# Attention and a two-layer network on one core: second parts of the first token columns on GpSimd, and the last weight ticks spread over four slots

## The chip, the core and the metric

The kernel runs on one core of one Trainium2 chip. The metric is device time in microseconds (us) of one launch. A core has five engines with a queue each: TensorE (PE in the profile; its weight loads are PEld), VectorE (DVE), ScalarE (ACT), GpSimd (POOL) and SyncE (SP), which here issues every DMA. Each engine works through its own list of instructions in order, and waits for the others through semaphores.

## What is computed

The reference is causal attention with a decay, and then a normalised two-layer network with a residual:

```python
# q, k, v: 8 batches x 8 heads x 576 tokens x 64; f: 8 x 8 x 576
scores = q @ k.T / 8 + cum[:, None] - cum[None, :]     # cum = cumsum(log f); causal mask
attn   = exp(scores - max) / (sum + 1e-9)
x      = (attn @ v)                                    # heads side by side: 8 x 576 x 512
xn     = (x - mean) / sqrt(var + 1e-6) * g_ln
out    = x + relu(xn @ w_ch1) @ w_ch2                  # 512 -> 2048 -> 512
```

The network's weights come as 64-bit floats, everything else as 32-bit floats.

## The kernel before

**Slots.** The attention is 64 heads of four slots each, slot `(n, t)` with t from 1 to 4, in all 256; a slot handles one tile of 128 query rows (t = 1 also a corner tile of 64). The body of a slot is a string of letters, one per piece of work, in the table `ORDERS`; the order of the letters is the order in which instructions are written out, and so their order on each engine. In slots 37 to 65 the string is (before that the same pieces stand in a somewhat other order, `R` near the end) `WwQSstAMhPelgNFrfmBDLRba`. The pieces that matter here are: `W` ticks of the weight preparation; `Q` scores on TensorE (L374); `S` mask and row minimum on VectorE (L409); `e` the exponential on ScalarE (L420); `B` the reciprocal of the row sum on VectorE (L425, L426) and the scaling of the row on GpSimd (L427); `t` the transposes on TensorE (L448) of the tile of two slots ago, which read what L427 wrote; `h` their copies on ScalarE (L504); `A` attention times values (L518); `F` copies of its result (L575, L576); `M` and `N` a step of the network's first and second layer on TensorE (L622 to L624, L644 to L646), with `r` and `m` the relu in two parts on ScalarE and VectorE (L630, L635); `P` preparation, `D` loads for later heads, `L` some steps of the reciprocal square root on GpSimd (L707 to L715), `R` the loads and splits of the network's token columns.

**Two-part numbers.** A 32-bit number is split for the matmuls into a first part (a rounded copy, by ScalarE) and a second part (the rest, by a subtraction). For the network's token columns `chunk_split` does this: L606 on ScalarE, then L607 on VectorE. A chunk is 256 tokens with four such column tiles `x_0` to `x_3`, and 16 steps of the first layer; chunk 0 is split at the ends of slots 36 and 37, and its first step is in slot 38. Two buffers `xr` hold the loaded columns, so the load of `x_2` waits until `x_0` is split.

**Weight preparation.** `WPrep` turns 32 pieces of weights (two layers, 16 each) into first and second parts, `w1h` with `w1l` and `w2h` with `w2l`. A tick moves every piece in work one step on. Per piece that is a load, a scaling on ScalarE (L166), three bit operations of 128x512 on VectorE (L182, L186, L189), for the first layer column sums on TensorE (L201) and four centring operations on VectorE (L209), then the first part on ScalarE (L225) and the second on GpSimd (L229). `W` runs ticks as they fall due: 0.8 per slot from slot 34 on. What is left in slot 56 (head 14, t = 1) is run there at once, in piece `P`, in a loop until all 37 ticks are done.

**Buffers.** The weight preparation's tiles are in a pool `early`. When it is done the pool is closed, and a pool `late` is opened in the same space; it holds the tiles of the heads from 16 on, which are split in two parts (`raw`, `hi`, `pw` and others). Heads 0 to 15 are computed in full precision and need none of it. TensorE's results go to banks of the PSUM memory; six banks of one tag are handed round among scores, transposes, products, column sums and first-layer steps, and a matmul waits until the bank that it gets has been read.

## Time and profile before

| what | value |
| --- | --- |
| device time, median of 3 runs | 1217.96 us (1214.26 to 1219.36) |
| the profiled execution's own time | 1217.98 us |
| its span, first to last instruction | 1216.1 us |
| mean granted TensorE clock | 0.993 |
| busy: TensorE, VectorE, ScalarE, GpSimd | 1190.1, 757.0, 619.3, 452.6 us |
| TensorE instructions (matmul) | 8368 |

The profiled execution's time is 1.9 us above its span and within 0.02 us of the median. In a row of the timeline or the chain the first number is the start in us, the second how long it took, then engine, line, operation, and the tiles it writes and reads; in square brackets stands how long the engine was idle before, and whose end ended that. A row of the table of windows has a stretch, its length, and for each engine the busy time in it with the number of instructions, then the clock granted to TensorE (1.00 is full speed), the share of the DMA engines and GB/s.

### The profile page before, as it was taken

What the parts mean: (1) busy time and instruction counts of PE and PEld (TensorE: products, weight loads), DVE (VectorE), ACT (ScalarE), POOL (GpSimd) and SP (SyncE); (2) the same over time, 40 slices, a digit from 0 to 9 for tenths busy, and PEclk for the clock granted to TensorE, in tenths of its full rate; (3) what the DMA queues carried; (4) which work ended last, traced back from release to release, by engine and by line L of the source; (5) the groups of instructions that cost most, each with busy time, mean ns of one, the idle gap of its engine ahead of it and who ended that gap; (6) DMA issues with size and microseconds to landing.
All of it is one profiled execution on the core that took longest, in us unless ns stands there. A gap on an engine that the chain in (4) does not pass through costs nothing.

```text
span 1216.1 us, 25716 instructions
## 1 busy us (share of the span) xinstructions
PE 1190.1 (98%) x8368; PEld 1068.3 (88%) x8368; DVE 757.0 (62%) x2664; ACT 619.3 (51%) x1936; POOL 452.6 (37%) x768
## 2 busy tenths in 40 slices
PE   8888998999999999999999999999999999999998
PEld 6557887899999989999999999999999999999997
DVE  6777683477777767777767676767677752222122
ACT  6886574555555555555555555556555541112111
POOL 3543344454444434454534344445444410000000
PEclk9998998999999999999999999999999999999999
DMA  6454452243434344434344444434444421111100
GB/s 192 142 153 151 127 148 63 87 133 131 139 125 143 123 141 131 146 129 135 124 129 141 129 135 131 143 120 139 132 132 131 128 86 41 31 36 39 31 26 27
DMA packets 127541, 139.00 MB, mean 114 GB/s; under 512 B 32432, under 2 KB 100016, under 8 KB 127408
## 3 DMA queue, kind: packets, MB, share of 16 engines
q1 hardware_dynamic: 127408, 137.36, 36.6%
q8 instruction: 67, 1.10, 0.4%
q14 instruction: 66, 0.54, 0.1%
HBM read 79.61 MB, written 19.17 MB: 81 GB/s over the span
## 4 chain that ended last, share of the span: by engine, by line
PE 91%; DVE 3%; ACT 2%; DMA 1%; issue 1%; POOL 1%; SPq 0%; DVEq 0%; ACTq 0%; POOLq 0%
PE h L622 12%; PE h L624 11%; PE h L623 11%; PE acc L644 11%; PE acc L645 11%; PE acc L646 11%; PE o L543 6%; PE tr L446 4%; PE s L376 3%; PE s L377 3%; PE s L374 2%; PE o L518 2%; PE tr L448 1%; ACT p L420 1%; DVE p L409 1%
## 5 line engine op out<-in xcount | busy, mean ns | idle before, releaser
L427 POOL TENSOR_SCALAR p<-p,st 64x64 f32<-64x64 f32 (+4 forms) x320 | 169.9, 532 | 511.5 <-ACT ph L504 232.4
L622 PE MATMUL h<-x,w1h 128*128 128x256 f32 x1152 | 342.3, 297 | 0.4 <-DVE st L409 0.4
L624 PE MATMUL h<-x,w1l 128*128 128x256 f32 x1152 | 326.8, 284 | 0.0
L623 PE MATMUL h<-x,w1h 128*128 128x256 f32 x1152 | 326.3, 283 | 0.0
L420 ACT ACTIVATE p<-p,st 64x64 f32<-64x64 f32 (+4 forms) x320 | 179.2, 561 | 210.6 <-DVE st L409 206.0
L635 DVE SCALAR_TENSOR_TENSOR hh<-h,hh 128x256 fp32r<-128x256 f32 x288 | 120.5, 418 | 194.4 <-ACT hh L630 192.0
L644 PE MATMUL acc<-w2h,hh 128*128 128x512 f32 x576 | 228.4, 397 | 0.0
L645 PE MATMUL acc<-w2l,hh 128*128 128x512 f32 x576 | 227.8, 396 | 0.0
L646 PE MATMUL acc<-w2h,hh 128*128 128x512 f32 x576 | 225.5, 391 | 0.0
L622 PEld LDWEIGHTS h<-x,w1h 128*128 128x128 f32 x1152 | 219.6, 191 | 5.3 <-issue 0.9
L623 PEld LDWEIGHTS h<-x,w1h 128*128 128x128 f32 x1152 | 220.6, 192 | 2.5
L624 PEld LDWEIGHTS h<-x,w1l 128*128 128x128 f32 x1152 | 220.3, 191 | 0.0
L630 ACT ACTIVATE hh<-h 128x256 fp32r<-128x256 f32 x288 | 109.9, 381 | 184.5 <-PE h L624 184.2
L409 DVE CUSTOM_DVE_ANT_0 p<-s,mask 64x64 f32<-64x64 f32 (+4 forms) x320 | 132.2, 421 | 26.4 <-PE s L377 17.7
L646 PEld LDWEIGHTS acc<-w2h,hh 128*128 128x128 f32 x576 | 108.5, 188 | 24.7
L425 DVE TENSOR_SCALAR st<-st 128x1 f32<-128x1 f32 (+1 forms) x320 | 47.7, 149 | 120.2 <-ACT p L420 117.2
L644 PEld LDWEIGHTS acc<-w2h,hh 128*128 128x128 f32 x576 | 109.5, 190 | 14.0 <-ACT ph_full L504 0.2
L645 PEld LDWEIGHTS acc<-w2l,hh 128*128 128x128 f32 x576 | 109.5, 190 | 11.7
L504 ACT CAST ph<-tr 64x128 fp32r<-64x128 f32 (+4 forms) x384 | 107.2, 328 | 3.6 <-PE tr L446 1.3
L579 ACT COPY ot<-o 64x320 f32<-64x320 f32 x96 | 38.0, 396 | 125.5 <-PE tr L446 63.7
L509 DVE TENSOR_TENSOR pl<-tr,ph 128x128 fp32r<-128x128 f32 x192 | 88.0, 458 | 4.3
L377 PE MATMUL s<-kl,xq 66*128 66x288 f32 (+4 forms) x288 | 83.2, 297 | 0.0
(89 smaller groups left out, 1888.7 us busy)
## 6 DMA issues: line engine op xcount, KB each, us to landing
raw<-in_qk_dram SPq DMA_DIRECT2D x96, 288.0 KB
wr<-in_w_dram SPq DMA_DIRECT2D x32, 512.0 KB
pw<-p SPq DMA_DIRECT2D x48, 288.0 KB
pw<-p SPq DMA_DIRECT2D x48, 224.0 KB
vr<-in_v_dram SPq DMA_DIRECT2D x64, 160.0 KB
out_dram<-xt SPq DMA_DIRECT2D x36, 256.0 KB
pw<-p SPq DMA_DIRECT2D x48, 160.0 KB
xa<-xs SPq DMA_DIRECT2D x32, 160.0 KB
```

The source lines that it names most:

```text
L377: mm(sp, xq, kl, start=False, stop=True)
L409: nc.vector.tensor_tensor_reduce(out=pt[:m, a:z], in0=sp, in1=mask[:m, off + a : off + z], scale=-SCALE, scalar=3.0e38 if i == 0 else st[: ...
L420: nc.scalar.activation(pt[:m, :w], pt[:m, :w], AF.Exp, bias=st[:m, i : i + 1], scale=-1.0, accum_out=st[:m, 2:3])
L427: nc.gpsimd.tensor_scalar(out=pt[:m, :w], in0=pt[:m, :w], scalar1=st[:m, 3:4], scalar2=1.0, op0=ALU.mult, op1=ALU.mult)
L622: mm(ph, w1h[:, k, fs], c.x[k][:, 0, :], start=(k == 0), stop=False)
L623: mm(ph, w1h[:, k, fs], c.x[k][:, 1, :], start=False, stop=False)
L624: mm(ph, w1l[:, k, fs], c.x[k][:, 0, :], start=False, stop=(k == KT - 1))
L630: nc.scalar.activation(h[:, 0, :], c.ph, AF.Relu)
L635: nc.vector.scalar_tensor_tensor(out=h[:, 1, :], in0=ph, scalar=0.0, in1=h[:, 0, :].bitcast(F32), op0=ALU.max, op1=ALU.subtract)
L644: mm(c.acc[i], h[:, 0, ts_], w2h[:, j, :], start=(j == 0), stop=False)
L645: mm(c.acc[i], h[:, 0, ts_], w2l[:, j, :], start=False, stop=False)
L646: mm(c.acc[i], h[:, 1, ts_], w2h[:, j, :], start=False, stop=(j == FT - 1))
```

## The change

`chunk_split` puts the subtraction on GpSimd as long as the pool `late` isn't open. The loop over the remaining ticks moves out of `P` of slot 56: piece `D` of slots 56, 57 and 58 now runs up to two ticks each, with all that they queue, and `D` of slot 59 runs what is left, closes `early`, opens `late` and issues the first of head 16's two `raw` loads. The second is issued in `D` of slot 60. Before, they were issued in `D` of slots 57 and 58.

```diff
+W_CLOSE = 2
...
         nc.scalar.copy(out=x[:, 0, :], in_=xr)
-        nc.vector.tensor_tensor(out=x[:, 1, :], in0=xr, in1=x[:, 0, :].bitcast(F32), op=ALU.subtract)
+        eng = nc.gpsimd if "late" not in pools else nc.vector
+        eng.tensor_tensor(out=x[:, 1, :], in0=xr, in1=x[:, 0, :].bitcast(F32), op=ALU.subtract)
...
         def next_raw():
 
-            if slot is not None and t in (2, 3) and NFULL <= n + 2 < B * H:
+            if slot is None:
+                return
+            if n == NFULL - 2:
+                ticks = W_CLOSE if t < 4 else 99
+                while not wp.done() and ticks > 0:
+                    wp.tick()
+                    wp.fill(99)
+                    ticks -= 1
+                if t == 4:
+                    early.close()
+                    pools["late"] = ctx.enter_context(tc.tile_pool(name="late", bufs=1))
+                    start_head(NFULL)
+                    load_raw(hd[NFULL], 1)
+            elif n == NFULL - 1 and t == 1:
+                load_raw(hd[NFULL], 0)
+            elif t in (2, 3) and NFULL < n + 2 < B * H:
                 if t == 2:
                     start_head(n + 2)
                 load_raw(hd[n + 2], 1 if t == 2 else 0)
...
                 if t == 1 and n + 1 < NFULL:
                     start_head(n + 1)
-                if n == NFULL - 2 and t == 1:
-                    while not wp.done():
-                        wp.tick()
-                        wp.fill(99)
-                    early.close()
-                    pools["late"] = ctx.enter_context(tc.tile_pool(name="late", bufs=1))
```

TensorE's list of instructions is the same before and after, row by row. On VectorE six subtractions of 128x256 go (chunk 0's four and chunk 1's first two), and they come up on GpSimd. The lines of the changed kernel stand one to two further down (L607 is now L609, L229 is L230, L427 is L428, L325 is L326, L723 is L725, L409 is L410, L182 is L183).

VectorE's list at the first split of chunk 0, from the end of slot 36 into slot 37; `st` are row statistics, `y_8` is a bit operation of the weights, `p_2` the masked scores of the tile `s_2`. Before:

```order
L425 TENSOR_SCALAR st_1_1348<-st_1_1348 128x1
L426 RECIPROCAL st_1_1348<-st_1_1348 128x1
L607 TENSOR_TENSOR x_0_1380<-xr_0_1326,x_0_1380 128x256
L607 TENSOR_TENSOR x_1_1383<-xr_1_1328,x_1_1383 128x256
L182 TENSOR_SCALAR y_8_1396<-wr_8_1264 128x512
L409 ISA p_2_1400,st_2_1401<-s_2_0_1398,mask 128x320
```

GpSimd's list at the same place in the changed kernel:

```order
L428 TENSOR_SCALAR p_1_1347<-p_1_1347,st_1_1348 128x192
L609 TENSOR_TENSOR x_0_1380<-xr_0_1326,x_0_1380 128x256
L609 TENSOR_TENSOR x_1_1383<-xr_1_1328,x_1_1383 128x256
L230 TENSOR_TENSOR w1l<-wy_6_989,w1h 128x4x128
L428 TENSOR_SCALAR p_2_1400<-p_2_1400,st_2_1401 128x320
L609 TENSOR_TENSOR x_2_1423<-xr_2_1386,x_2_1423 128x256
L609 TENSOR_TENSOR x_3_1426<-xr_3_1388,x_3_1426 128x256
L230 TENSOR_TENSOR w2l<-wy_7_1243,w2h 128x512
```

VectorE goes from the reciprocal straight to the bit operation and the scores of `s_2`; on GpSimd each pair of subtractions stands behind a row scaling and ahead of a weight's second part.

GpSimd's list where the weight preparation ends, from slot 56 on; `rs` are steps of the reciprocal square root. Before:

```order
L229 TENSOR_TENSOR w2l<-wy_14_2224,w2h 128x512
L229 TENSOR_TENSOR w1l<-wy_14_2138,w1h 128x4x128
L229 TENSOR_TENSOR w2l<-wy_15_2329,w2h 128x512
L229 TENSOR_TENSOR w1l<-wy_15_2285,w1h 128x4x128
L427 TENSOR_SCALAR p_0_175<-p_0_175,st_0_2436 64x64
L427 TENSOR_SCALAR p_1_2438<-p_1_2438,st_1_2439 128x192
L712 TENSOR_TENSOR rs_2154<-rs_2154 128x2
```

The same place in the changed kernel:

```order
L230 TENSOR_TENSOR w2l<-wy_14_2224,w2h 128x512
L428 TENSOR_SCALAR p_0_175<-p_0_175,st_0_2436 64x64
L428 TENSOR_SCALAR p_1_2438<-p_1_2438,st_1_2439 128x192
L230 TENSOR_TENSOR w1l<-wy_14_2138,w1h 128x4x128
L230 TENSOR_TENSOR w2l<-wy_15_2329,w2h 128x512
...
L428 TENSOR_SCALAR p_2_2490<-p_2_2490,st_2_2491 128x320
L230 TENSOR_TENSOR w1l<-wy_15_2285,w1h 128x4x128
```

The row scalings of slot 56 now stand behind one second part in place of four; the last second part, `w1l` of piece 15, stands behind the row scaling of slot 57 and six `rs` steps. ScalarE's `L225` for piece 15 likewise moves from ahead of slot 56's exponentials to behind them.

SyncE's list of DMAs from slot 57 on, `xb` being a store of attention's result, `vr` a load of values and `out_dram` the store of chunk 0. Before:

```order
L325 DMA raw_1_2528<-in_qk_dram 128x576
L332 DMA vr_2566<-in_v_dram 128x5x64
L325 DMA raw_0_2583<-in_qk_dram 128x576
L592 DMA xb_156<-xs_320_2377 128x256
L723 DMA out_dram<-xt_0_2151 128x512
L723 DMA out_dram<-xt_1_2394 128x512
L341 DMA kl_2720<-cumd 2x576
```

In the changed kernel:

```order
L333 DMA vr_2560<-in_v_dram 128x5x64
L593 DMA xb_156<-xs_320_2377 128x256
L326 DMA raw_1_2622<-in_qk_dram 128x576
L725 DMA out_dram<-xt_0_2151 128x512
L725 DMA out_dram<-xt_1_2394 128x512
L326 DMA raw_0_2689<-in_qk_dram 128x576
L342 DMA kl_2720<-cumd 2x576
```

Both `raw` loads stand later, the second one now behind the two stores of chunk 0.

## The prediction

> **What bounds it now.** I read first the page's busy times and the granted clock, then the table of windows for the first 203 us, in which the change lies.

> ```profile
> PE 1190.1 (98%) x8368; PEld 1068.3 (88%) x8368; DVE 757.0 (62%) x2664; ACT 619.3 (51%) x1936; POOL 452.6 (37%) x768
> core 0: 1216.1 us, clock 0.993
> 0.00:203.20 203.20, 181.42 (x1259) 142.86 (x1260) 144.50 (x517) 139.22 (x426) 87.07 (x137) 0.96 0.49 143
> ```

> TensorE bounds the kernel: it is busy 98% of the span. Of its 26.0 us of idle time, 21.8 (203.20 - 181.42) lie in the first 203 us; after that it is idle 4.2 us in 1013. The clock is 0.96 in this stretch. So an edit pays if it lets TensorE reach 203 us earlier, and what it gains there arrives at the end. The change touches two places before 203 us and nothing that TensorE waits for later.

> A clock of 0.993 is a loss of 8.5 us of full-speed time (0.007 x 1216.1). The windows, cut where the clock steps, show where:

> ```profile
> 93.99:97.40 3.41, 2.39 (x14) 1.65 (x13) 3.23 (x14) 2.49 (x7) 1.56 (x2) 0.99 0.35 93
> 97.40:100.81 3.41, 3.41 (x22) 3.03 (x20) 2.60 (x11) 2.37 (x8) 1.93 (x2) 0.51 0.71 212
> 100.81:104.23 3.42, 1.52 (x10) 0.88 (x7) 2.91 (x8) 3.38 (x11) 2.19 (x4) 0.99 0.53 146
> 104.23:107.64 3.41, 2.67 (x7) 1.86 (x8) 3.38 (x12) 1.81 (x5) 0.56 (x1) 0.50 0.69 212
> 107.64:111.05 3.41, 3.41 (x25) 3.01 (x24) 2.87 (x7) 1.75 (x5) 1.48 (x2) 0.51 0.41 137
> 189.55:192.96 3.41, 0.98 (x4) 0.26 (x3) 1.27 (x7) 1.43 (x6) 3.41 (x4) 0.99 0.13 48
> 192.96:196.38 3.42, 2.66 (x19) 2.06 (x20) 0.00 (x0) 1.14 (x4) 2.93 (x12) 0.50 0.31 86
> 196.38:199.79 3.41, 3.41 (x19) 3.08 (x16) 0.00 (x0) 0.52 (x2) 0.18 (x1) 0.51 0.35 93
> ```

> Three times a window of 3.41 us with little TensorE work (2.39, 1.52, 0.98 us busy) is followed by half clock: one window the first time, two windows the second and third, since the window after the drop is itself not full (2.67, 2.66). Five windows at half are 17.1 us, or 8.5 lost, which is all of it. The second and third are the two places of the change, and each hangs on one wait. I call them A (chunk 0's first split) and B (the end of the weight preparation).

> **A, the split on GpSimd.** The chain of waits at 102 us, and TensorE's timeline:

> ```profile
> 101.79 0.44 PE tr L448 x4
> 102.23 0.12 PE tr_4b L448
> 102.43 1.48 DVE x L607
> 103.91 0.60 DVE y L182
> 104.52 0.39 DVE p L409
> ...
> 104.97 1.86 PE L374 MATMUL s<-kl,xf 66*128 66x448 f32 x2 [2.63 <-DVE st L409]
> ...
> 111.25 0.38 PE L622 MATMUL h<-x,w1h 128*128 128x256 f32 x1
> ```

> TensorE waits 2.63 us for the masking of `s_2` (L409), which stands on VectorE behind two L607 and an L182. Their times:

> ```profile
> 101.45 0.16 DVE L426 RECIPROCAL st<-st 128x1 f32<-128x1 f32 x1
> 102.06 1.85 DVE L607 TENSOR_TENSOR x<-xr,x 128x256 fp32r<-128x256 f32 x2 [0.44 <-ACT x L606]
> 103.83 0.68 DVE L182 TENSOR_SCALAR y<-wr 128x512 uint32<-128x512 uint32 x1
> ...
> 102.20 1.43 POOL L229 TENSOR_TENSOR w1l<-wy,w1h 128x512 fp32r<-128x512 f32 x1
> 107.08 0.80 POOL L427 TENSOR_SCALAR p<-p,st 128x320 f32<-128x320 f32 x1 [3.45 <-DVE st L426]
> L607 DVE TENSOR_TENSOR x<-xr,x x72: 411/424/1484, 102.1 to 1164.6; 128x256 fp32r<-128x256 f32 x72
> ```

> Without the two L607, L182 starts when the reciprocal ends, at 101.61 in place of 103.83: 2.22 us sooner, the 0.44 of waiting included. Then `s_3` starts at 102.75 instead of 104.97, TensorE idles 0.4 us, and the window to 104.23 holds 2.95 us of work (1.52 + 1.43). The drops above came after 2.39 us and less (the windows with 2.67 and 2.66 were at half already), so I take it that the clock stays full. The work from 104.97 to 111.25, 6.28 us at half, then takes half of that, 3.14. The bounds of A: 2.2 us if the clock falls all the same for as long, 5.4 (2.22 + 3.14) if nothing else is late. Not all will be on time: the column sum's readers (L209) stand behind the reciprocal of slot 37, which waits for ScalarE, and the product L518 waits on VectorE. ScalarE is full in that window (3.38 of 3.42). I take off 1.0 for that: **A = 4.4 us**.

> What moves to GpSimd costs there, per 128x256 subtraction, an estimate between 0.72 (half of the 128x512 subtraction at 102.20, 1.43) and 1.43 (a whole one); nothing of this form is on GpSimd now. I take 0.72, since twice the elements should be twice the work. Two of them fill 102.2 to 103.7 and push `w1l` there to about 105.1; GpSimd idles 3.45 us before its next row scaling, so that is hidden. The second pair comes behind that scaling, at about 106 to 107.4 on the new clock, and the first step's matmuls reach `x_2` and `x_3` 0.8 and 1.2 us after their start at 106.8: on time by some tenths. If that cover is gone, each tenth costs TensorE a tenth. The load of `x_2`, which waits for the split of `x_0`, is issued 0.4 us later, that of `x_3` a little sooner. Chunk 1's two subtractions (0.42 us each by the last row) I count at nothing: they come after the half clock of A, where VectorE has room (2.87 of 3.41 us).

> [...]

> **B, the ticks spread.** GpSimd, TensorE and what TensorE takes at full speed for the same kinds of work:

> ```profile
> 188.42 1.30 POOL L229 TENSOR_TENSOR w2l<-wy,w2h 128x512 fp32r<-128x512 f32 x1
> ...
> 192.12 1.26 POOL L229 TENSOR_TENSOR w1l<-wy,w1h 128x512 fp32r<-128x512 f32 x1
> 193.36 0.71 POOL L427 TENSOR_SCALAR p<-p,st 64x64 f32<-64x64 f32 x2
> ...
> 195.59 0.53 POOL L427 TENSOR_SCALAR p<-p,st 128x320 f32<-128x320 f32 x1
> 189.61 0.92 PE L374 MATMUL s<-kl,xf 66*128 66x448 f32 x2
> 193.72 1.04 PE L448 MATMUL tr<-identr,p 128*64 128x128 f32 x3 [3.20 <-POOL p L427]
> ...
> 197.03 0.58 PE L622 MATMUL h<-x,w1h 128*128 128x256 f32 x1
> ...
> 199.75 0.40 PE L644 MATMUL acc<-w2h,hh 128*128 128x512 f32 x1
> ...
> 202.37 0.36 PE L622 MATMUL h<-x,w1h 128*128 128x256 f32 x1
> ```

> TensorE wants slot 56's rows at 190.53 and gets them at 193.72, since their scaling stands behind four L229. In the change one L229 is ahead: the scalings run at 189.7 to 190.4, before TensorE asks. That removes 3.20 us of idle time; and the work from 193.72 to 199.75, 6.03 us at half clock, takes 3.0. So the next second-layer matmul comes at about 193.6 in place of 199.75. I take **B = 6.0 us**, between 3.2 (the clock falls all the same) and 6.2.

> What is late next: the second parts themselves. `w1l` of piece 14 ends at 191.7, and the step that needs it comes at 192.2 (190.53 and half of the 3.31 us from 193.72 to 197.03). `w1l` of piece 15 stands behind six `rs` steps (194.04 to 195.59 now, 1.55 us) and slot 57's scaling (0.53): 190.4 + 2 x 1.26 + 1.55 + 0.53 + 1.26 = 196.3, and step 15 comes at 196.2 (193.6, and the 2.62 us from 199.75 to 202.37), its third matmul, the first to read `w1l`, some 0.2 later. Slot 57's scaling ends at 195.0, and its transposes come just ahead of step 15. All hold, the tightest by a tenth. ScalarE's two casts (L225) go behind slot 56's exponentials, which come sooner for it; the steps that read what they write are two slots away and more. VectorE's four L209 likewise change places with four short row operations.

> The loads: SyncE now holds `raw_1` behind a store and `raw_0` behind the two stores of chunk 0.

> ```profile
> 193.40 0.33 SPq L325 DMA_DIRECT2D raw<-in_qk_dram  x1
> 197.76 0.62 SPq L325 DMA_DIRECT2D raw<-in_qk_dram  x1
> 210.45 1.00 SPq L723 DMA_DIRECT2D out_dram<-xt  x2
> 211.95 0.68 ACT L342 CAST hi<-raw 128x576 fp32r<-128x576 f32 x1
> 215.71 0.67 ACT L348 CAST hi<-raw 128x576 fp32r<-128x576 f32 x1
> ```

> `raw_1` can't be issued before the last `w1l` ends (196.3), and ScalarE reads it about 6 us before 211.95, that is at 206. `raw_0` follows the stores at 211.5 on the old clock and is read at 215.71: 4.2 us for 800 KB with the stores' 512, or 190 GB/s, where windows above moved 212 (their last number). So this holds with little to spare, at no cost; uncovered, ScalarE would wait a microsecond, with two slots between it and TensorE. The loads and stores that they are moved past (`vr`, `xb`) only go sooner.

> **The sum.** Profiled execution 1217.98 - 4.4 - 6.0 = 1207.6; with three tenths for the tight places, **1208 us**. The median of the runs is the same as this execution's time, so no correction.

> **Rivals.** (1) *The clock falls at A all the same* (0.12). For it: the first drop came after a window with as much as 2.39 us. It would cost 1.7 (one window at half) to 3.1 of A: 1209.5 to 1211. [...]

> (2) *VectorE takes A's gain back* (0.13): it is busy in 2.9 to 3.4 us of each window at A, and if it bounds the stretch up to 186 us, only B is left: 1212. Against it: at 107.64 to 111.05 it already has room (2.87 of 3.41). (3) *The last second parts take the stall's place* (0.1): if `w1l` 15 is over a microsecond late, step 15 waits, and a window may go to half: B shrinks to 2 to 4, 1210 to 1213. (4) *It doesn't matter* (0.05): TensorE finds both waits again behind ScalarE: 1216 to 1219. (5) *Slower* (0.04): `raw_0` lands so late behind the stores that ScalarE stops, with the exponentials behind it, and TensorE runs dry with the clock at half behind it. It decides once the landing is more than two slots late (about 10 us, by the 5.3 us between the two L622 under B); to end above 1224 it has to cost 16 us beyond that, a landing after about 241 on the old clock. No row shows a load that slow.

> **Chances.** The forecast has 0.56. I call faster what is below 1211.9 (0.5%, 6.1 us, about what a measurement here can tell from no change): the forecast, rival 1 and half of rivals 2 and 3, 0.79, less 0.03 for what I don't see: 0.76. Same 0.19: the rest of 2 and 3, rival 4, and 0.02 of that. Slower 0.05: rival 5 and 0.01 of it. The range is 1204 (both gains at their upper bounds, 5.4 + 6.2, and two more for a third clock drop that a shifted phase avoids) to 1213.5 (B alone with its clock half kept).

> **What would show it.** Right: no idle time of over 1 us before TensorE's L374 and L448 near 103 and 190; a granted clock of 0.998 to 0.999, with one half window left; GpSimd's split near 0.7 us; the first L622 near 106.8, the L644 near 189; the same 4 us of idle time after that. Wrong: half clock behind 104; a wait of TensorE for GpSimd at L623 or L624; a wait of ScalarE for `raw`.

## The result, and the profile after

The changed kernel takes 1208.47 us (median of 6 runs, 1207.64 to 1213.36) against 1217.47 for the kernel before, run beside it. The ratio is 0.9941, with a 95% interval of 0.9919 to 0.9963. The prediction was 1208.0. The profiled execution took 1208.30 us, where that of before took 1217.98.

The page's busy times, the clock, and the windows that answer to those of before:

```profile
PE 1187.0 (98%) x8368; PEld 1066.3 (88%) x8368; DVE 752.9 (62%) x2658; ACT 619.4 (51%) x1936; POOL 456.6 (38%) x774
```

```profile
core 0: 1206.5 us, clock 0.997
```

```profile
0.00:203.20 203.20, 188.35 (x1329) 149.86 (x1330) 145.81 (x529) 145.50 (x446) 93.32 (x148) 0.98 0.50 145
203.20:1206.50 1003.30, 998.69 (x7041) 916.45 (x7039) 607.12 (x2129) 473.87 (x1491) 363.23 (x627) 1.00 0.35 109
104.20:111.10 6.90, 6.86 (x58) 5.91 (x58) 5.65 (x17) 6.11 (x19) 5.29 (x8) 1.00 0.84 282
185.00:215.00 30.00, 30.00 (x219) 25.18 (x217) 12.36 (x53) 15.93 (x53) 14.75 (x25) 1.00 0.26 79
```

In the first 203.2 us TensorE is idle 14.9 us in place of 21.8, and has 70 more matmuls done (1329 against 1259). After that it is idle 4.6 us (1003.30 - 998.69), nearly as before (4.2). Behind A, from 104 to 111 us, the clock is full, where it was at half (0.50 and 0.51); around B TensorE isn't idle at all.

**A.** The timelines of TensorE, GpSimd and VectorE in the changed kernel, and GpSimd's of the kernel before for the row scaling one slot earlier:

```profile
103.36 1.02 PE L375 MATMUL s<-kl,xf 66*128 66x448 f32 x2 [0.69 <-DVE st L410]
...
107.08 0.39 PE L624 MATMUL h<-x,w1h 128*128 128x256 f32 x1
```

```profile
99.62 0.74 POOL L428 TENSOR_SCALAR p<-p,st 128x576 f32<-128x576 f32 x1 [2.79 <-ACT w1h L226]
...
102.92 1.42 POOL L609 TENSOR_TENSOR x<-xr,x 128x256 fp32r<-128x256 f32 x2
...
106.65 1.42 POOL L609 TENSOR_TENSOR x<-xr,x 128x256 fp32r<-128x256 f32 x2 [0.46 <-ACT x L607]
```

```profile
102.15 0.16 DVE L427 RECIPROCAL st<-st 128x1 f32<-128x1 f32 x1
102.23 0.68 DVE L183 TENSOR_SCALAR y<-wr 128x512 uint32<-128x512 uint32 x1
102.82 0.48 DVE L410 CUSTOM_DVE_ANT_0 p<-s,mask 128x320 f32<-128x320 f32 x1
```

```profile
98.88 0.75 POOL L427 TENSOR_SCALAR p<-p,st 128x576 f32<-128x576 f32 x1 [2.79 <-ACT w1h L225]
```

VectorE goes from the reciprocal straight to the bit operation and the masking, and TensorE's 2.63 us of idle time is 0.69. A split on GpSimd takes 0.71 us (1.42 for two). The second pair ends at 108.07, and TensorE, which starts the step at 107.08, has no gap. The first L622 of before, at 111.25, is now the L624 at 107.08: 4.17 us sooner. The execution was already 0.74 us later one slot ahead (99.62 against 98.88), so in this pair of executions A brought 4.17 + 0.74 = 4.91 us.

**B.** GpSimd and TensorE, then SyncE's loads and ScalarE's casts of them:

```profile
184.41 1.29 POOL L230 TENSOR_TENSOR w2l<-wy,w2h 128x512 fp32r<-128x512 f32 x1
185.69 0.71 POOL L428 TENSOR_SCALAR p<-p,st 64x64 f32<-64x64 f32 x2
...
190.39 0.53 POOL L428 TENSOR_SCALAR p<-p,st 128x320 f32<-128x320 f32 x1
190.89 1.28 POOL L230 TENSOR_TENSOR w1l<-wy,w1h 128x512 fp32r<-128x512 f32 x1
```

```profile
186.36 0.50 PE L449 MATMUL tr<-identr,p 128*64 128x128 f32 x3
...
189.57 0.40 PE L646 MATMUL acc<-w2h,hh 128*128 128x512 f32 x1
...
192.50 0.28 PE L626 MATMUL h<-x,w1l 128*128 128x256 f32 x1
```

```profile
200.26 1.00 SPq L725 DMA_DIRECT2D out_dram<-xt  x2
201.30 0.44 SPq L326 DMA_DIRECT2D raw<-in_qk_dram  x1
```

```profile
201.76 0.68 ACT L343 CAST hi<-raw 128x576 fp32r<-128x576 f32 x1
...
205.14 0.47 ACT L505 COPY ph_full<-tr 64x192 f32<-64x192 f32 x2 [1.88 <-PE tr L449]
205.51 0.67 ACT L349 CAST hi<-raw 128x576 fp32r<-128x576 f32 x1
```

Slot 56's row scalings follow the one remaining second part, and the transposes (L449) show no idle time in front: the 3.20 us are gone. From the first network step to the second-layer matmul it was 88.50 us (199.75 - 111.25) and is 82.49 (189.57 - 107.08): 6.01 less, where 6.0 was predicted. The last `w1l` ends at 192.17, and its reader, step 15's third matmul, starts at 192.50. ScalarE's casts of `raw_1` (201.76) and of `raw_0` (205.51, whose load was issued last, at 201.30) show no idle time in front.

### The profile page after: what moved, and what is told of

Same layout as the page of the kernel before. It is cut to its first block, busy times and chain, and to the rows that moved or that the text cites. A ratio compares the mean times of both kernels' runs of the same rounds, so it can differ in the third digit from the quotient of the medians.

```text
span 1206.5 us, 25720 instructions
## 1 busy us (share of the span) xinstructions
PE 1187.0 (98%) x8368; PEld 1066.3 (88%) x8368; DVE 752.9 (62%) x2658; ACT 619.4 (51%) x1936; POOL 456.6 (38%) x774
## 4 chain that ended last, share of the span: by engine, by line
PE 91%; DVE 3%; ACT 2%; DMA 1%; issue 1%; POOL 0%; SPq 0%; DVEq 0%; POOLq 0%; ACTq 0%
PE h L624 12%; PE h L626 11%; PE h L625 11%; PE acc L646 11%; PE acc L647 11%; PE acc L648 11%; PE o L544 6%; PE tr L447 4%; PE s L377 3%; PE s L378 3%; PE s L375 2%; PE o L519 2%; PE tr L449 1%; DVE p L410 1%; PE pc L202 1%
## 5 line engine op out<-in xcount | busy, mean ns | idle before, releaser
L428 POOL TENSOR_SCALAR p<-p,st 64x64 f32<-64x64 f32 (+4 forms) x320 | 169.6, 531 | 497.5 <-ACT ph L505 246.7
L624 PE MATMUL h<-x,w1h 128*128 128x256 f32 x1152 | 341.7, 297 | 0.4 <-DVE st L410 0.4
L646 PE MATMUL acc<-w2h,hh 128*128 128x512 f32 x576 | 228.4, 397 | 0.0
L624 PEld LDWEIGHTS h<-x,w1h 128*128 128x128 f32 x1152 | 219.0, 190 | 5.3 <-issue 0.9
L410 DVE CUSTOM_DVE_ANT_0 p<-s,mask 64x64 f32<-64x64 f32 (+4 forms) x320 | 132.3, 421 | 26.2 <-PE s L378 17.4
L426 DVE TENSOR_SCALAR st<-st 128x1 f32<-128x1 f32 (+1 forms) x320 | 47.7, 149 | 121.3 <-ACT p L421 118.2
L646 PEld LDWEIGHTS acc<-w2h,hh 128*128 128x128 f32 x576 | 109.4, 190 | 14.0 <-issue 0.2
```

Of the source, the lines that this page charges most:

```text
L410: nc.vector.tensor_tensor_reduce(out=pt[:m, a:z], in0=sp, in1=mask[:m, off + a : off + z], scale=-SCALE, scalar=3.0e38 if i == 0 else st[: ...
L428: nc.gpsimd.tensor_scalar(out=pt[:m, :w], in0=pt[:m, :w], scalar1=st[:m, 3:4], scalar2=1.0, op0=ALU.mult, op1=ALU.mult)
L624: mm(ph, w1h[:, k, fs], c.x[k][:, 0, :], start=(k == 0), stop=False)
L646: mm(c.acc[i], h[:, 0, ts_], w2h[:, j, :], start=(j == 0), stop=False)
```

## The experiments

All ratios are to the kernel before, run beside the other on the same chip. Every run also lists its mean TensorE clock, and it differs from run to run of one kernel: the 26 runs of the kernel before beside the repeat run reached from 1212.37 us (clock 0.999) to 1220.82 (0.990). So I also give each kernel's time at full clock. It comes from one straight line through all 166 runs, with a level for each kernel and a common slope, 0.77 us per 0.001 of clock; the runs scatter about it by 1.1 us. Two kernels of six runs each then compare to about 0.7 us (one standard error, so a difference of 1 us may be chance). All but the first of these kernels were run in three groups, each with its own runs of the kernel before: A alone, B alone in both forms and the two-input work (29 runs of before); the repeat, the fillers and the one-input work (26); the rest (12). Before's own level is 1212.9, 1211.8 and 1211.9 us in them, so across groups a level is uncertain by another 1 us. These levels are estimates, and the ratios are the measurements.

| kernel | median us (runs) | ratio [95%] | mean clock | us at full clock |
| --- | --- | --- | --- | --- |
| before, all runs | | 1 | 0.9937 (67) | 1212.3 |
| changed | 1208.47 (6) | 0.9941 [0.9919, 0.9963] | 0.9963 | 1206.4 |
| changed, again | 1208.62 (6) | 0.9937 [0.9917, 0.9958] | 0.9970 | 1206.4 |
| A alone | 1214.74 (12) | 0.9978 [0.9964, 0.9991] | 0.9948 | 1211.0 |
| B alone | 1209.65 (6) | 0.9937 [0.9915, 0.9959] | 0.9977 | 1208.5 |
| B alone, all ticks in slot 56 | 1212.20 (12) | 0.9952 [0.9934, 0.9971] | 0.9954 | 1208.7 |
| A and B, all ticks in slot 56 | 1208.16 (7) | 0.9939 [0.9917, 0.9960] | 0.9973 | 1206.7 |
| B's wait filled with transposes | 1212.25 (12) | 0.9975 [0.9961, 0.9988] | 0.9976 | 1210.9 |
| B's wait filled with matmuls | 1215.51 (12) | 0.9987 [0.9970, 1.0005] | 0.9952 | 1211.1 |
| changed, two-input work back on VectorE | 1211.70 (12) | 0.9944 [0.9924, 0.9963] | 0.9950 | 1208.4 |
| changed, one-input work on VectorE | 1209.87 (9) | 0.9955 [0.9936, 0.9973] | 0.9960 | 1207.2 |
| changed, no addition of 1e-9 | 1202.80 (5) | 0.9894 [0.9870, 0.9919] | 0.9978 | 1201.6 |

### The two parts by themselves

A alone is the kernel before with the split's engine chosen:

```diff
-        nc.vector.tensor_tensor(out=x[:, 1, :], in0=xr, in1=x[:, 0, :].bitcast(F32), op=ALU.subtract)
+        eng = nc.gpsimd if "late" not in pools else nc.vector
+        eng.tensor_tensor(out=x[:, 1, :], in0=xr, in1=x[:, 0, :].bitcast(F32), op=ALU.subtract)
```

> Only the split of the first token columns goes to GpSimd; the last ticks stay in one loop in slot 56. My theory (two separate stalls, each with two windows at half clock behind it, that add up): 1217.5 - 4.4 = 1213.1 us, ratio 0.996 to 0.997; full clock from 104 on, the 3.2 us wait near 186 and its two half windows still there. Rival (the gain at the split is given back before 186 us, VectorE being the bound there): no change, 1217, with new idle time of TensorE between 111 and 186 us. Rival (the two are not independent): less than 2 us.

B alone is the changed kernel with all splits on VectorE:

```diff
-        eng = nc.gpsimd if "late" not in pools else nc.vector
-        eng.tensor_tensor(out=x[:, 1, :], in0=xr, in1=x[:, 0, :].bitcast(F32), op=ALU.subtract)
+        nc.vector.tensor_tensor(out=x[:, 1, :], in0=xr, in1=x[:, 0, :].bitcast(F32), op=ALU.subtract)
```

> Only the last ticks are spread and the late pool is opened in slot 59; the split stays on VectorE. My theory: 1217.5 - 6.0 = 1211.5 us, ratio about 0.995; two half windows left near 104, none near 193. Rival (the stall at the split alone makes the difference): no change. Rival (the gain of the spread is larger than the sum said): under 1210.

The third is the kernel before with the loop over the ticks only moved within slot 56, from `P` to `D`, all ticks still in one place:

```diff
         def next_raw():
 
+            if slot is not None and n == NFULL - 2 and t == 1:
+                while not wp.done():
+                    wp.tick()
+                    wp.fill(99)
+                early.close()
+                pools["late"] = ctx.enter_context(tc.tile_pool(name="late", bufs=1))
...
-                if n == NFULL - 2 and t == 1:
-                    while not wp.done():
-                        wp.tick()
-                        wp.fill(99)
-                    early.close()
-                    pools["late"] = ctx.enter_context(tc.tile_pool(name="late", bufs=1))
```

> All the last ticks stay in slot 56, but behind the row scalings of that slot (in the piece that loads) and not ahead of them; pool opened there and both raw loads issued as before; split on VectorE. Tells the spreading over four slots from the mere place behind slot 56's scalings. My theory (what counts is that slot 56's row scaling stands ahead of the subtractions): slot 56's wait goes; three second parts in a row then delay slot 57's scaling by one more subtraction, 1.3 us, to about 196.3, where its transposes want it at about 196, so a wait of up to 1 us and the clock stays full: 1211.5 to 1212.5 us. Rival (the spread over slots is needed): a wait of 2 us or more moves to slot 57's transposes, half clock again, 1214 to 1217.

A alone brings 2.7 us (0.0022 of 1217.6; interval 1.1 to 4.4). B alone brings 7.7 (0.0063 of 1217.6; 5.0 to 10.3), and with all ticks in slot 56 5.8 (0.0048 of 1217.6; 3.5 to 8.0). In the profile of A alone the clock is full behind A, and the wait at B stands as before, with half clock; the timeline of TensorE at B and the windows:

```profile
189.92 1.04 PE L448 MATMUL tr<-identr,p 128*64 128x128 f32 x3 [3.21 <-POOL p L427]
```

```profile
104.20:107.60 3.40, 3.34 (x33) 2.76 (x33) 3.25 (x11) 2.70 (x8) 2.83 (x5) 1.00 0.73 219
189.00:195.70 6.70, 5.78 (x33) 4.85 (x34) 0.00 (x0) 1.65 (x6) 3.26 (x12) 0.51 0.31 77
```

The profile of B alone was to show A's wait and half clock behind it. It shows another picture; VectorE's, GpSimd's and TensorE's timelines, and the windows with the wait and behind it:

```profile
101.88 0.76 DVE L608 TENSOR_TENSOR x<-xr,x 128x256 fp32r<-128x256 f32 x2
```

```profile
101.88 1.25 POOL L428 TENSOR_SCALAR p<-p,st 64x64 f32<-64x64 f32 x2 [0.65 <-ACT x L607]
```

```profile
103.69 1.02 PE L375 MATMUL s<-kl,xf 66*128 66x448 f32 x2 [1.37 <-DVE st L410]
```

```profile
101.80:105.20 3.40, 2.03 (x13) 1.42 (x12) 3.40 (x10) 3.30 (x9) 2.49 (x3) 1.00 0.66 156
105.20:108.60 3.40, 3.40 (x37) 3.06 (x36) 3.32 (x11) 2.10 (x7) 2.05 (x2) 1.00 0.83 268
```

The order of these instructions is that of the kernel before, but the two subtractions took 0.76 us and not 1.85, and the 0.44 us of waiting for ScalarE ahead of them aren't there. This time GpSimd's row scaling beside them was the slow one, 1.25 us where the changed kernel has 0.71. TensorE waited 1.37 us in place of 2.63, and full clock followed. So A's price isn't a constant of the code: the 1.85, and the half clock, were what one execution showed. Three more of the profiles below have the split on VectorE: all ticks in slot 56, the transposes as filler, and the matmuls as filler. Their rows of TensorE for the same wait are

```profile
103.56 1.02 PE L374 MATMUL s<-kl,xf 66*128 66x448 f32 x2 [1.54 <-DVE st L409]
```

```profile
103.44 1.02 PE L374 MATMUL s<-kl,xf 66*128 66x448 f32 x2 [1.37 <-DVE st L409]
```

```profile
103.76 1.86 PE L374 MATMUL s<-kl,xf 66*128 66x448 f32 x2 [1.37 <-DVE st L409]
```

So the wait was 1.37 to 1.54 us in four of five executions and 2.63 in one, and half clock followed in two of the five, the profile of before and the one with matmuls.

Moving the loop as a whole does what spreading it does, as far as these runs tell: at full clock 1208.7 against 1208.5. The wait of up to 1 us that was expected at slot 57 isn't there: TensorE is idle 0.14 us from 185 to 215 us. GpSimd's timeline:

```profile
185.79 0.71 POOL L427 TENSOR_SCALAR p<-p,st 64x64 f32<-64x64 f32 x2
186.47 1.27 POOL L229 TENSOR_TENSOR w1l<-wy,w1h 128x512 fp32r<-128x512 f32 x1
```

Slot 56's scalings stand ahead of the other three second parts. That counts; the spread over four slots and the later `late` pool show no gain of their own. ScalarE's casts (L225) and VectorE's four L209 have moved behind slot 56's row work too, so this run alone doesn't single out GpSimd. The profile of before does, in VectorE's last reciprocal of slot 56:

```profile
188.96 0.17 DVE L426 RECIPROCAL st<-st 128x1 f32<-128x1 f32 x1
```

The row statistics were ready at 189.13, over a microsecond before TensorE wanted the rows (190.53), while GpSimd ran its four second parts without a gap until the scaling at 193.36.

### The changed kernel again, and both parts with the ticks in one place

The first is the changed kernel unaltered. The second is the kernel of the last diff with the split's engine chosen as in A alone.

> The changed kernel once more, beside the others, for its time and its clock over more runs. Theory (its gain is two waits gone, worth 6.5 us at equal clock, and fewer half windows): 1208 to 1209.5 us, mean clock 0.996 to 0.998 against 0.993 of the kernel before; runs with the same clock as a run of the kernel before are still 6 us faster. Rival (only the clock differs): runs of equal clock have equal times.

> Split on GpSimd as in the changed kernel, but all last ticks in slot 56 behind its row scalings, pool opened there and both raw loads issued as before. My theory (the place behind the scalings is what counts, the spread adds nothing): the changed kernel's time, 1208 to 1209.5 us, and the same at equal clock. Rival (without the spread slot 57's scaling comes too late): 1 to 3 us more, with a wait of TensorE for GpSimd near 192.

The repeat gives 0.9937 [0.9917, 0.9958], the other 0.9939 [0.9917, 0.9960], and at full clock they are 0.3 apart. What A adds on top of B is too small for the ratios: 0.9937 for B alone against 0.9941 and 0.9937 for both. At full clock it is 2.1 us (1208.5 - 1206.4), and with the ticks in one place 2.0 (1208.7 - 1206.7). Both compare across groups of runs; if B's kernels are set lower by the 1 us by which before stands higher in their group, about 1 us is left.

### What the clock costs at B

The kernel before, with work put into TensorE's wait at B, so that the wait stays and only the idle time goes: 28 transposes of an identity matrix, or 25 matmuls of the network's form. Their results are read by nobody.

```diff
+    def filler(u):
+        warm = bank(f"warmf{u}")
+        for _ in range(28):
+            nc.tensor.transpose(warm[:, 0:P], ident, ident)
...
+            if c == "t" and slot == (NFULL - 2, 3):
+                filler(u)
```

```diff
+        for _ in range(25):
+            mm(warm[:, 0:C], w1h[:, 0, 0:P], w2h[:, 0, 0:C], start=True, stop=True)
```

> The kernel before, with 28 transposes of the identity, into a bank that nothing reads, ahead of slot 58's transposes, where TensorE waited 3.2 us. The wait stays, the work in it is for nothing. Theory 1 (any TensorE work counts for the clock): no half windows behind that place, and 2 to 3 us less than before, 1214.5 to 1215.5 us, with the same time at equal clock. Theory 2 (transposes don't count for the clock): half clock there as before, 1217 to 1218 us.

> The same with 25 matmuls of 128x128 by 128x256 in place of the transposes. Theory 1 and theory 2 both: no half windows behind that place, 1214.5 to 1215.5 us. Rival (the half clock there costs nothing, being hidden): 1217 to 1218 us.

The transposes bring 3.0 us (1.5 to 4.7 by the interval). TensorE's timeline with them, and the window behind:

```profile
186.34 3.22 PE L812 MATMUL warmf<-identr 128*128 128x128 f32 x28
189.73 0.81 PE L448 MATMUL tr<-identr,p 128*64 128x128 f32 x3 [0.17 <-POOL p L427]
```

```profile
189.70:195.70 6.00, 5.87 (x44) 4.79 (x45) 0.92 (x4) 2.04 (x7) 3.00 (x11) 1.00 0.51 149
```

GpSimd is as late as before, and the clock behind the wait is full (1.00). So B has two terms, the wait (3.2) and the clock behind it (3.0 predicted, 3.0 measured, 1.5 to 4.7), and it is the idle time that brings the clock down there. The matmuls as filler also leave full clock behind B in their profile, but their median brings only 1.6 us (-0.6 to 3.6). That profile has half clock at 39 us (0.50) and at A (0.53 from 104 to 110.9 us), where the code is that of before; the mean clock of its 12 runs is 0.9952 against 0.9976 with transposes, and at full clock the two kernels are 0.2 us apart. So the difference between the medians is a difference of mean clock, in the profile half clock in other places. Why the twelve runs had it oftener stays open; what differs between the two profiles at A stands in the last section.

The second theory, that transposes don't count for the clock, fails: these 28, of 32-bit floats as this kernel issues them, do. Nothing else fills those 3.2 us, and the clock behind them stays at 1.00, where the kernel before has 0.50 and 0.51.

### What occupies VectorE at A

The changed kernel, with work given back to VectorE at the first split, while the split itself stays on GpSimd: two subtractions of two inputs, or two statistics instructions of one input, into a scratch tile.

```diff
+        if c.n == 0 and k < 2:
+            nc.vector.tensor_tensor(out=scrap, in0=xr, in1=x[:, 0, :].bitcast(F32), op=ALU.subtract)
```

```diff
+        if c.n == 0 and k < 2:
+            nc.vector.bn_stats(scrap[:, 0:6], xr)
```

> The changed kernel, with two extra subtractions of 128x256 on VectorE, into a tile that nothing reads, where the first pair of chunk 0's split stood before. GpSimd has the real ones. Theory 1 (VectorE's queue time ahead of the masking is what TensorE waits for, and a subtraction with two SBUF inputs is held up by GpSimd's subtraction beside it): the extra pair takes 1.8 us or more in place of 0.85, TensorE waits 2.5 us or more at the next scores, half clock follows: 1208.5 + 4 = 1212 to 1213. Theory 2 (what helped was something else, as the order of GpSimd's work): 1208.5 to 1209.

> The changed kernel with two extra statistics instructions of 128x256 on VectorE (one SBUF input each) where the two extra subtractions stood. Theory 1 (a subtraction with two SBUF inputs and GpSimd's own hold each other up, one with one input doesn't): the pair takes 0.75 us and GpSimd's pair its 1.4 us; TensorE waits 0.7 us longer, the clock mostly stays full: 1209 to 1210 us, at equal clock 0.7 us above the changed kernel. Theory 2 (GpSimd's work beside it slows VectorE whatever the operands): as with the two subtractions, 1211 to 1213 us, and a pair of 1.3 us or more.

VectorE, GpSimd and TensorE in the profile with two inputs:

```profile
102.40 1.33 DVE L613 TENSOR_TENSOR scrap<-xr,x 128x256 f32<-128x256 f32 x2 [0.43 <-ACT x L609]
```

```profile
102.55 1.76 POOL L611 TENSOR_TENSOR x<-xr,x 128x256 fp32r<-128x256 f32 x2
```

```profile
104.78 1.86 PE L375 MATMUL s<-kl,xf 66*128 66x448 f32 x2 [2.23 <-DVE st L410]
```

And with one input:

```profile
101.54 0.87 DVE L613 BATCH_NORM_STATS2 scrap<-xr 128x6 f32<-128x256 f32 x2
```

```profile
101.55 0.71 POOL L428 TENSOR_SCALAR p<-p,st 64x64 f32<-64x64 f32 x2 [0.64 <-DVE st L426]
102.23 1.41 POOL L611 TENSOR_TENSOR x<-xr,x 128x256 fp32r<-128x256 f32 x2
```

```profile
103.45 1.02 PE L375 MATMUL s<-kl,xf 66*128 66x448 f32 x2 [1.47 <-DVE st L410]
```

With two inputs TensorE's wait is back (2.23), half clock too (a mean of 0.81 from 100 to 120 us; the first score matmuls take 1.86 and not 1.02), and both engines are slower: VectorE 1.33 for two in place of 0.76, GpSimd 1.76 in place of 1.42. More was expected, 1.8 us for the pair and a wait of 2.5. With one input GpSimd is no slower (0.71 and 1.41), but that pair ran beside GpSimd's row scaling (where with the two-input pair of B alone it took 1.25) and met GpSimd's subtractions for only 0.18 us (102.23 to 102.41). So whether one-input work would hold up the subtractions is not tested. At full clock the two-input work makes the changed kernel as slow as B alone beside it (1208.4 against 1208.5), so it takes back all that A had brought; the one-input work costs 0.8, about the length of its two instructions. So VectorE's time ahead of the masking is what TensorE waits for, and some 0.6 us of it (1.33 - 0.76) came while both engines ran two-input subtractions. The medians alone don't separate these two kernels from the changed one: the intervals overlap.

### VectorE's time elsewhere

If TensorE waits in the opening for the row chain that VectorE is part of, and for nothing after it, work taken off that chain in every slot pays in the opening alone. The softmax adds 1e-9 to a row sum that holds exp(0) = 1, which changes nothing in 32 bits; here the addition is dropped and the reciprocal reads the sum:

```diff
-        nc.vector.tensor_scalar_add(st[:m, 3:4], st[:m, 2:3], 1e-9)
-        nc.vector.reciprocal(st[:m, 3:4], st[:m, 3:4])
+        nc.vector.reciprocal(st[:m, 3:4], st[:m, 2:3])
```

> The changed kernel without the addition of 1e-9 to the row sums (320 instructions of 0.15 us on VectorE); the reciprocal reads the sum itself. A row sum is at least 1, where an addition of 1e-9 changes no bit of a 32-bit float, so nothing that is computed changes. Theory (before slot 37 TensorE waits for the row chain that VectorE is part of, after it for nothing): TensorE idles 3 us less in the first 100 us, nothing changes after 203 us, 1205 to 1206.5 us, 2 to 3 us below the changed kernel, at equal clock too. Rival (ScalarE or the loads bound that stretch): no change, 1208.5 us. Rival (the 320 x 0.15 us = 48 us count everywhere): far below 1200.

It takes 1202.80 us (1201.85 to 1206.13), ratio 0.9894 [0.9870, 0.9919], so it beats both kernels, the changed one by some 5.4 to 5.8 us of medians and 4.8 at full clock (1206.4 - 1201.6). That is about twice what I expected. Windows up to the first network step, of this kernel and then of the changed one:

```profile
0.00:101.12 101.12, 89.56 (x643) 66.22 (x643) 73.66 (x256) 81.11 (x252) 49.69 (x82) 1.00 0.60 173
```

```profile
0.00:107.08 107.08, 93.08 (x643) 68.58 (x643) 80.80 (x304) 82.18 (x254) 49.63 (x82) 0.97 0.57 163
```

The same 643 matmuls are done 5.96 us sooner, and the span is 6.3 shorter (1200.2 against 1206.5): nearly all of it is gained before the network begins. VectorE is busy 7.1 us less there. TensorE is idle 2.4 us less (11.56 against 14.00) and busy 3.5 less, with the clock at 1.00 and not 0.97; how much of that clock is chance, this pair of profiles doesn't tell. In the rest of the span VectorE loses another 41 us of work (of 48.5 in all, 704.4 against 752.9), which bring a few tenths. VectorE isn't full in the opening, 75% busy in the changed kernel (80.80 of 107.08): TensorE's waits there are short ones, the most for GpSimd's row scaling (3.7 us in 10 waits up to 100 us), which stands behind the dropped instruction. So it is the length of the chain that paid, or VectorE's time in it; the two were not separated.

## Why the prediction was right, and where it wasn't

**What bounds the kernel: right.** What TensorE gains before 203 us arrives at the end: it was 10.2 us ahead at B (199.75 to 189.57), and the span is 9.6 shorter.

**B: right, term by term.** 6.0 was predicted; the pair of profiles gives 6.01, and the runs of B alone 7.7 (5.0 to 10.3) and, with all ticks in slot 56, 5.8 (3.5 to 8.0), two kernels 0.2 us apart at full clock. The clock's 3.0 was measured apart, with the transposes. The tight places held: the last `w1l` is 0.33 us ahead of its reader, where a tenth was predicted for step 15, and the L646 comes at 189.57 where "near 189" stood. That it needed the spread over four slots was not claimed, and it didn't.

**A: the mechanism right, the size wrong.** The wait was VectorE's time ahead of the masking, and the second pair was on time. GpSimd's split took 0.71 us (0.72 predicted, from half of a 128x512 subtraction that was itself slow: 1.43, where the median of its kind is 1.27 and a half would be 0.64). It is 1.7 times VectorE's median of 0.424. In the pair of profiles A is 4.17, or 4.91 with the lag upstream taken out, so 4.4 looks confirmed. The runs say 2.7 (1.1 to 4.4) for A alone; at full clock it is 1.3 alone (1212.3 - 1211.0; 1.9 against the 29 runs of before beside it) and 1 to 2 on top of B, so under the lower bound of 2.2, with the rest hanging on the clock. The step that failed is the one that took 3.14 us of half clock, and the 2.22 us with the slowed subtraction in it, as fixed parts of that place. The profile of before was one draw, and the odd one of five: with the same order of instructions on VectorE and GpSimd at A, four other executions waited 1.37 to 1.54 us, and three of them had no half clock behind it. The wait that goes is then 0.7 to 0.85 us (down to 0.69), and half clock goes in two executions of five. The row of 1484 ns against a median of 424 stood in the prediction, and was taken as the rule of that place.

**The sum: so close partly by luck, two errors that offset.** At full clock the change brings 5.9 us (1212.3 - 1206.4), and the mean clock rises from 0.9937 to 0.9966, which at 0.77 us per 0.001 is 2.2 more: 8.1 in all. The prediction had 10.0. By the ratios the runs give 7.2 (4.5 to 9.9) and 7.7 (5.1 to 10.1), so it was about 2 us high, and that is A. It started too high as well: the profiled execution of before, 1217.98 at clock 0.993, lies 0.9 above that kernel's mean run (1212.3 + 0.77 x 6.3 = 1217.1). Together with the scatter of 1.1 us this brings the time within 0.5 us of the forecast.

**The clock: wrong in its detail.** I expected 0.998 to 0.999 and one half window. The profile has 0.997 and two, both upstream of the change, where the code is as before; windows of the changed kernel:

```profile
38.40:41.70 3.30, 3.26 (x16) 2.89 (x18) 2.38 (x13) 1.61 (x5) 1.05 (x2) 0.50 0.85 234
93.10:96.50 3.40, 3.40 (x21) 2.84 (x21) 3.09 (x11) 2.68 (x10) 2.07 (x3) 0.51 0.40 139
```

The kernel before had no half clock at 38 (1.00 from 36 to 46 us), and the changed one has. Behind A and B it has none (1.00), as predicted.

**The rivals.** (1), the clock falling at A all the same, didn't happen in any of the six profiles with the split on GpSimd and nothing of two inputs put back on VectorE; as a statement about the average it comes near, since part of A's clock gain wasn't there to be had. (2), only B left at 1212, fell as a time, but its point holds in part: with B alone 1209.65 are reached, and A's share is 1 to 2. (3), (4) and (5) weren't seen: no wait at step 15, both idle times gone or down to 0.69, no wait for `raw`.

## What to carry to other kernels

Look at what stands in a helper engine's queue ahead of the one instruction that the bottleneck waits for: here the place of the bulk work in that queue counted, and spreading it added nothing that could be seen (1208.5 us at full clock with the spread, 1208.7 without). A gain that rests on half clock is a gain in the average over runs: take it from several runs that list their clock, not from the windows of one. An instruction far above its own median, like the 1484 ns here, is the same warning. Work taken off an engine paid only in the stretch where TensorE waited for a chain through that engine (7.1 us of VectorE's time up to the first network step went with 5.96 us gained, another 41 us after it with a few tenths), so there the small instructions of every slot are worth a look.

## What the runs showed of the hardware

```profile
100.19:103.60 3.41, 1.51 (x7) 0.79 (x7) 3.24 (x10) 3.37 (x13) 2.77 (x4) 1.00 0.70 198
103.60:107.01 3.41, 3.25 (x10) 2.43 (x11) 3.38 (x13) 2.16 (x8) 1.97 (x3) 0.50 0.80 267
```

```profile
101.65:105.06 3.41, 2.04 (x13) 1.43 (x12) 3.41 (x11) 3.31 (x10) 2.47 (x3) 1.00 0.69 184
105.06:108.48 3.42, 3.42 (x37) 3.08 (x36) 3.28 (x12) 2.12 (x8) 2.05 (x2) 1.00 0.81 265
```

  With 1.51 us of work in the window half clock follows, with 2.04 it doesn't. At A 1.52 (before) and 1.71 (two-input work) are followed by half clock too, and 2.19 (B with all ticks in slot 56) isn't. This is no threshold for other places: the first drop of before followed a window with 2.39. What the slowest runs of before lose to half clock is about 10 us of 1217, an estimate from 0.013 of clock at 0.77 us per 0.001, and the change that was to be measured is no larger.
- **A loss of clock wasn't a loss of time one to one.** Half clock's 0.001 would be 1.22 us of this span, and the runs show 0.77. That early half windows run partly in time in which TensorE waits anyway would explain it; that was not tested by itself. Half clock behind B seems to cost more than the slope: with the wait filled by transposes or matmuls the time at full clock is 1.4 and 1.2 us below before's, though the wait itself is still there. Against the 26 runs of before beside them it is 1.0 and 0.7, so this is an indication only.
- **VectorE and GpSimd took longer beside each other, in either direction.** A two-input subtraction beside GpSimd's took 1484 ns in one run, where the median is 424 (and GpSimd's 1.43 us, where the median is 1.27), in another GpSimd's scaling took 1.25 in place of 0.71, and in a third both lost some (1.33 for 0.76, 1.76 for 1.42). One-input work on VectorE left GpSimd's scaling beside it at 0.71; beside GpSimd's subtraction it was not tested for more than 0.18 us.
- **Transposes alone kept the clock full**, over 3.2 us (28 of 128x128, clock 1.00 in the 6 us behind them).
